# Three of every 24 high-part casts of a maxout MoE layer, cast by VectorE instead of ScalarE

## The chip, the cores and the metric

The kernel runs on one core of one Trainium2 chip. The metric is the device time of one execution in microseconds (us), the median of three runs. Five engines work side by side, each through its own queue in order: TensorE (PE, with its weight loads as PEld), VectorE (DVE), ScalarE (ACT), GpSimd (POOL) and SyncE (SP, which issues DMAs here).

## The reference

Four batches of 12,544 tokens with 128 channels go through attention over 32 inducing points, and then through a maxout layer:

```python
h = mab(I, x)          # 32 inducing points attend to the tokens
attn_out = mab(x, h)   # the tokens attend to the 32 results
x = attn_out.reshape(B * S, D)
h = np.maximum(np.maximum(x @ w1, x @ w2), x @ w3)   # 768 wide
return h @ w_out
```

`mab(q, kv)` is softmax(q kvT / sqrt(128)) kv. All of it is fp32.

## The kernel before

**What is computed.** The maximum is taken as x w2 + max(0, x (w1 - w2), x (w3 - w2)), so that x w2 w_out is one product with a 128 x 128 matrix. Since x itself is (probabilities) times a 32 x 128 matrix per batch, that small matrix is multiplied with all weights first (`us`, one per batch), and the tokens enter only through their transposed softmax probabilities `pT`, split in a high and a low part to keep fp32 accuracy.

**Tiling.** A batch has seven groups of tokens: a short one and six full ones of 16 x 128 tokens (groups 1 to 6). A full group is four chunks of 512 tokens. For each chunk the 768 hidden channels are six blocks of 128. One block of one chunk is a *slot*; a full group is a window of 24 slots, numbered 0 to 23 here (slot = 6 x chunk + block), and the kernel has 600 slots, 24 full windows among them. "b2 group 3" is the window of group 3 of the third batch; batches count from 0.

**One slot** passes through five engines' queues:
- PE multiplies `pu` (L790) and `pv` (L800) into PSUM, each of two banks in turn.
- ScalarE writes `ru` = max(0, pu) into SBUF (L809), which frees the bank of `pu`.
- VectorE writes `h` = max(pv, ru) (L830, from five buffers in turn), which frees the bank of `pv`.
- The high part `hi` of `h`, rounded to the type fp32r that PE reads in one pass, is a cast: on ScalarE (L819), or on VectorE (L817) for the slots of the whole kernel listed in `HIVEC` (0, 2, 4 and 7).
- The low part `lows` = h - hi is a subtraction: on POOL (L827), or on VectorE (L833) for the slots of a window listed in `LOWVEC` (23, 0, 15, 18; in the last batch `LOWLAST`, with 9 too; b0 group 1 only 23).
- Six slots later PE adds hi wo_hi, hi wo_lo and lows wo_hi into the chunk's accumulator (L862 to L864; one more product, L861, opens a chunk). After its sixth block ScalarE copies the chunk out of PSUM (L875) and SP stores it.

**What sets the order.** The order of each queue is the order in which the program calls the engines. `main()` walks over the slots; step s calls `advance()`, then what `plan[s]` holds, then `stage2()` for slot s - 6. `advance()` at step s issues pu of slot s + 1, pv of slot s, ru of s + 1, the high cast of slot s - 1, its low part on POOL, h of slot s, and last a low part that VectorE takes over from the step before. So the high cast of a slot stands just ahead of the next slot's h where VectorE does it, and behind the ru two slots on where ScalarE does it. `plan[s]` holds the rest of the work: the softmax of the coming group's probabilities in ten steps on VectorE and ScalarE (`STEPS2`, among them the exp of step 8 at L716, the division of step 11, the transposition of step 13 at L739 and the copy `ph` of step 14 at L742), and the attention of the inducing points of the next batch (products L366 and L502 in bursts on PE, exp L449, maxima L404 and L434, transposition L478). Batch 3 has no next batch, so there this attention is missing.

Of the kernel before, what the change touches and what calls it, by code (L numbers as in the profile page):

```python
# [25 lines left out]
def kernel(ctx, tc, x, xt, ind_t, w1, w2, w3, w_out, out):  # L26
# [6 lines left out]
    NJ = DF // P  # L33
# [85 lines left out]
    )  # L119
    LOWVEC = (23, 0, 15, 18)  # L120
    LOWLAST = (23, 0, 9, 15, 18)
    UW = 2 * DF + C
    UQ = UW // NQ

# [100 lines left out]
    wf = xtp.tile([P, 2, DF], F32, name="wf", tag="xT")  # L225
    wcat = const.tile([P, UW], F32, name="wcat")
    wo_hi = const.tile([P, NJ, C], F32R, name="wo_hi")
# [7 lines left out]
    def convert(k, step):  # L235

        v = raws[k].rearrange("p (k two) -> p two k", two=2)
        low, high = v[:, 0, :], v[:, 1, :]
        c = parts[k]
        if step == "t":  # L240
# [12 lines left out]
        elif step == "r":  # L253

            c["rest"] = temp(F32, "rest")
            nc.vector.scalar_tensor_tensor(
                out=c["rest"], in0=low, scalar=2.0**-52, in1=c["pw"].bitcast(F32), op0=ALU.mult, op1=ALU.mult
            )
        elif step == "z":

            c["size"] = temp(F32, "size")
            nc.scalar.activation(out=c["size"], in_=high.bitcast(F32), func=AF.Square)
        elif step in "Aa":
            (nc.gpsimd if step == "A" else nc.vector).tensor_add(out=c["rest"], in0=c["rest"], in1=c["t"].bitcast(F32))
        elif step == "d":

            c["dst"] = wf[:, k, :] if k < 2 else temp(F32, "dst")
            size, rest, dst = c["size"], c["rest"], c["dst"]
            if k != 1:

                size, rest = (v.rearrange("p (n two) -> p two n", two=2) for v in (size, rest))
                dst = dst.rearrange("p (two n) -> p two n", two=2)
            nc.vector.scalar_tensor_tensor(
                out=dst, in0=size, scalar=LEAST * LEAST, in1=rest, op0=ALU.is_ge, op1=ALU.mult
            )
        elif step == "S":
            nc.gpsimd.tensor_sub(
                out=wcat[:, : 2 * DF].rearrange("p (j s c) -> p s j c", s=2, c=P)[:, k - 2],
                in0=c["dst"].rearrange("p (j c) -> p j c", c=P),
                in1=wf[:, 0, :].rearrange("p (j c) -> p j c", c=P),  # L280
            )
# [333 lines left out]
    def first_products(st, which, bank):  # L615
        if which == 0:
            st["us"] = bp.tile([P, UW], F32R, name="us", tag="us")
            st["up"] = {}
        cs = slice(512 * which, min(UW, 512 * which + 512))
        up = bank[:, : cs.stop - cs.start]  # L620
# [25 lines left out]
    def combine_products(st, bank):  # L646
        st["us"] = bp.tile([P, UW], F32R, name="us", tag="us")
        st["up"] = bank
        for k in range(NQ):
            nc.tensor.matmul(  # L650
                out=bank[k * M : (k + 1) * M, :],
                lhsT=st["hT"][:, :M],
                rhs=wcat[:, k * UQ : (k + 1) * UQ],
                start=True,
                stop=True,
            )
# [20 lines left out]
    def turned(ap):  # L677

        return ap.rearrange("p (a b) -> p b a", a=2)

    def sorted_(ap):

        return ap.rearrange("p (b a) -> p a b", a=2)

    def halves(ap):

        return ap.rearrange("p (a b) -> p a b", a=2)
# [93 lines left out]
    HIVEC = (0, 2, 4, 7)  # L781

    def advance():

        s = pipe["next"]
        pipe["next"] += 1
        if s + 1 < len(slots):
            c, j = slots[s + 1]
            pu, w = bank_u[(s + 1) % 2], c.w
            nc.tensor.matmul(  # L790
                out=pu[:, :w],
                lhsT=state[c.b]["us"][:, 2 * j * P : (2 * j + 1) * P],
                rhs=turned(c.pT[:, :w]),
                start=True,
                stop=True,
            )
        if 0 <= s < len(slots):
            d, j = slots[s]
            pv = bank_v[s % 2]
            nc.tensor.matmul(  # L800
                out=pv[:, : d.w],
                lhsT=state[d.b]["us"][:, (2 * j + 1) * P : (2 * j + 2) * P],
                rhs=turned(d.pT[:, : d.w]),
                start=True,
                stop=True,
            )
        if s + 1 < len(slots):
            ru = hp.tile([P, 512], F32, name="ru", tag="ru", bufs=3)
            nc.scalar.activation(out=halves(ru[:, :w]), in_=sorted_(pu[:, :w]), func=AF.Relu)  # L809
            relus[s + 1] = ru  # L810
        low = pipe.pop("low", None)
        if 0 <= s - 1 < len(slots):
            c, j = slots[s - 1]
            h = sums.pop(s - 1)
            hi = hp.tile([P, 512], F32R, name="hi", tag="hi", bufs=10)
            if s - 1 in HIVEC:
                nc.vector.tensor_copy(out=hi[:, : c.w], in_=h[:, : c.w])  # L817
            else:
                nc.scalar.copy(out=hi[:, : c.w], in_=h[:, : c.w])  # L819
            lo = lows[:, (s - 1) % NL, :]  # L820
            c.hh.append(hi)
            c.hl.append(lo)
            args = dict(out=lo[:, : c.w], in0=h[:, : c.w], in1=hi.bitcast(F32)[:, : c.w])
            if c.low(j):
                pipe["low"] = args
            else:
                nc.gpsimd.tensor_sub(**args)  # L827
        if 0 <= s < len(slots):
            h = hp.tile([P, 512], F32, name="h", tag="h", bufs=5)
            nc.vector.tensor_max(out=halves(h[:, : d.w]), in0=sorted_(pv[:, : d.w]), in1=halves(relus.pop(s)[:, : d.w]))  # L830
            sums[s] = h
        if low:
            nc.vector.tensor_sub(**low)  # L833

    class Chunk:
# [7 lines left out]
        def low(self, k):  # L843

            if self.q is None or (self.gi == 1 and self.q == k == 0):
                return False
            if self.b == 0 and self.gi == 1:
                return NJ * self.q + k in LOWVEC[:1]
            return NJ * self.q + k in (LOWVEC if self.b + 1 < B else LOWLAST)

    def stage2(c, j):
        us = state[c.b]["us"]
        w = c.w
        if j == 0:
            c.acc = [(bank_o[c.n % 2], slice(0, w))]
            if c.n == len(chunks) - 1:
                c.acc = [(bank_a[k], slice(k * w // 2, (k + 1) * w // 2)) for k in range(2)]
        for acc, cs in c.acc:
            to = acc[:, : cs.stop - cs.start]
            if j == 0:  # L860
                nc.tensor.matmul(out=to, lhsT=us[:, 2 * DF :], rhs=turned(c.pT[:, cs]), start=True, stop=False)  # L861
            nc.tensor.matmul(out=to, lhsT=wo_hi[:, row_of(j), :], rhs=turned(c.hh[j][:, cs]), start=False, stop=False)  # L862
            nc.tensor.matmul(out=to, lhsT=wo_lo[:, row_of(j), :], rhs=turned(c.hh[j][:, cs]), start=False, stop=False)  # L863
            nc.tensor.matmul(out=to, lhsT=wo_hi[:, row_of(j), :], rhs=turned(c.hl[j][:, cs]), start=False, stop=(j == NJ - 1))  # L864
# [65 lines left out]
    def begins(win):  # L930
        b, g = divmod(win - 1, NG - 1)
        return b * per_batch + short + g * WIN

    for win, slot, kind, n, gi in MOVES:
        s = begins(win) + slot
# [39 lines left out]
    for n, turns in enumerate(TURNS, start=1):  # L975
        for gi, win, slot, wait, past in turns:
            s = begins(win) + slot
# [9 lines left out]
        s = begins(win) + (8 if slot < 8 else 20)  # L987
# [9 lines left out]
    def main():  # L997
        over = None
        for s in range(len(slots) + LAG + 1):

            if s >= LAG:
                spare[0] = bank_o[((s - LAG) // NJ + 1) % 2]
            if pipe["next"] <= s:
                advance()
            k = s // NJ + AHEAD
            if s % NJ == 4 and k < len(chunks):
                chunks[k].pT = probs(chunks[k])
            if over:
                finish(over)
                over = None  # L1010
            if s == len(slots) + LAG:
                break
            for f, args in plan[s]:
                f(*[state[a[1]] if isinstance(a, tuple) and a[0] == "state" else a for a in args])
            if s >= LAG:
                c, j = slots[s - LAG]
                stage2(c, j)
                if j == NJ - 1:
                    over = c

    def first(step, st):
# [18 lines left out]
            "eg": lambda: attend_products(1, 2, bank_a[1]),  # L1040
            "ek": lambda: keep_scores(1),
            "s": advance,
            "a": lambda: next(steps["a"]),
            "b": lambda: next(steps["b"]),
# [107 lines left out]
```

## Time and profile before

| what | value |
|---|---|
| median of three runs | 789.8 us (789.71 to 789.95) |
| the profiled execution's own time | 790.35 us |
| its span, first to last instruction | 788.5 us, granted TensorE clock 0.999 |
| busy share of the span | PE 98%, ACT 92%, DVE 81%, POOL 81%, PEld 79% |
| high casts on ScalarE, L819 | 596, of 128 x 512 elements 575 |
| high casts on VectorE, L817 | 4 |
| low parts on POOL, L827, and on VectorE, L833 | 504 and 96 |

A busy share counts overlapping instructions once; matmuls are pipelined, so that a PE which is always busy may still lose time between the starts of its matmuls. The rows below give an instruction's start in us from the span's start, its duration, engine, line, operation and operands. An engine's next instruction may start a little before the one ahead is over.

### The profile page before, as it was taken

To read this page: it belongs to the slowest core of one execution; us is meant where nothing else is said; L and a number is where in the kernel's file an instruction comes from. 1 tells how busy PE (TensorE), PEld (TensorE's weight loads), DVE (VectorE), ACT (ScalarE), POOL (GpSimd) and SP (SyncE) were. 2 spreads that over 40 slices of the span, in tenths; PEclk is the share of its full clock that TensorE was granted. 3 is DMA by queue.
4 is the path that set the end of the run, shared out by engine and by line. 5 is a ranking of instruction groups with operands and counts; after the bars stand their busy time and mean duration, and the time that the engine had idled before them with its cause. 6 is when DMAs were issued, how large, how long until landed. Compare 5 with 4: busy or idle time off the path is not lost.

```text
span 788.5 us, 14348 instructions
## 1 busy us (share of the span) xinstructions
PE 774.7 (98%) x4567; PEld 626.4 (79%) x4567; DVE 639.4 (81%) x1071; ACT 727.1 (92%) x1529; POOL 639.6 (81%) x523
## 2 busy tenths in 40 slices
PE   8999999999999999999999999999999999999998
PEld 6768878878787787787878877878888788787887
DVE  5898978878877787887887878878888788888876
ACT  5789899999998999998998999999999999999996
POOL 1379879878788897887987978879879989888887
PEclk9999999999999999999999999999999999999999
DMA  9744325274542643543644336334223222222221
GB/s 355 293 148 126 100 91 178 62 249 161 189 139 65 200 131 101 188 123 108 217 137 132 114 103 195 120 114 134 71 79 96 74 81 81 68 87 73 69 81 53
DMA packets 52266, 102.24 MB, mean 130 GB/s; under 512 B 18144, under 2 KB 21344, under 8 KB 46944
## 3 DMA queue, kind: packets, MB, share of 16 engines
q1 hardware_dynamic: 52048, 101.21, 40.5%
q8 instruction: 36, 0.59, 0.3%
q14 instruction: 38, 0.31, 0.1%
q10 hardware_dynamic: 144, 0.13, 0.0%
HBM read 48.12 MB, written 25.69 MB: 94 GB/s over the span
## 4 chain that ended last, share of the span: by engine, by line
PE 56%; ACT 33%; POOL 3%; DMA 3%; DVE 2%; issue 1%; SPq 0%; POOLq 0%; ACTq 0%; DVEq 0%
ACT ru L809 14%; ACT hi L819 13%; PE pu L790 10%; PE acc L862 9%; PE pv L800 9%; PE acc L863 9%; PE acc L864 9%; PE aux L696 3%; POOL lows L827 3%; ACT o L875 2%; PE acc L502 2%; DMA raw<-in_w_dram 2%; PE aux L366 2%; PE acc L861 2%; ACT aux L449 1%
## 5 line engine op out<-in xcount | busy, mean ns | idle before, releaser
L827 POOL TENSOR_TENSOR lows<-h,hi 128x512 fp32r<-128x512 f32 (+1 forms) x504 | 624.4, 1275 | 112.4 <-ACT hi L819 109.3
L830 DVE TENSOR_TENSOR h<-pv,ru 128x512 f32<-128x512 f32 (+1 forms) x600 | 400.9, 673 | 123.8 <-PE pv L800 63.0
L809 ACT ACTIVATE ru<-pu 128x512 f32<-128x512 f32 (+1 forms) x600 | 407.0, 679 | 37.8 <-PE pu L790 37.5
L819 ACT CAST hi<-h 128x512 fp32r<-128x512 f32 (+1 forms) x596 | 416.3, 699 | 0.3 <-DVE h L830 0.2
L790 PE MATMUL pu<-pT,us 128*128 128x512 f32 (+1 forms) x600 | 229.2, 382 | 4.5 <-ACT ru L809 3.7
L800 PE MATMUL pv<-pT,us 128*128 128x512 f32 (+1 forms) x600 | 226.6, 378 | 1.6 <-DVE h L830 1.5
L862 PE MATMUL acc<-hi,wo_hi 128*128 128x512 f32 (+1 forms) x594 | 225.5, 380 | 0.0
L863 PE MATMUL acc<-hi,wo_lo 128*128 128x512 f32 (+1 forms) x594 | 222.6, 375 | 0.0
L864 PE MATMUL acc<-lows,wo_hi 128*128 128x512 f32 (+1 forms) x594 | 222.6, 375 | 0.0
L790 PEld LDWEIGHTS pu<-pT,us 128*128 128x128 f32 x600 | 113.2, 189 | 37.8 <-ACT ru L809 18.8
L862 PEld LDWEIGHTS acc<-hi,wo_hi 128*128 128x128 f32 x594 | 112.2, 189 | 21.9 <-issue 7.5
L800 PEld LDWEIGHTS pv<-pT,us 128*128 128x128 f32 x600 | 113.4, 189 | 19.6 <-DVE h L830 6.6
L864 PEld LDWEIGHTS acc<-lows,wo_hi 128*128 128x128 f32 x594 | 112.3, 189 | 15.3
L863 PEld LDWEIGHTS acc<-hi,wo_lo 128*128 128x128 f32 x594 | 112.3, 189 | 14.7
L833 DVE TENSOR_TENSOR lows<-h,hi 128x512 fp32r<-128x512 f32 x96 | 87.7, 913 | 0.8 <-ACT hi L819 0.8
L875 ACT COPY o<-acc 128x512 f32<-128x512 f32 (+1 forms) x96 | 65.3, 680 | 0.0
L861 PE MATMUL acc<-pT,us 128*128 128x512 f32 (+1 forms) x99 | 37.3, 376 | 0.0
L502 PEld LDWEIGHTS acc<-xg,aT 128*32 128x32 f32 x640 | 18.0, 110 | 9.6 <-issue 5.4
L696 PE MATMUL aux<-xT,hT 128*32 128x512 f32 x192 | 25.1, 603 | 0.0
L366 PE MATMUL aux<-xT,iT 128*32 128x512 f32 x184 | 24.1, 596 | 0.2 <-ACT pT L768 0.2
L502 PE MATMUL acc<-xg,aT 128*32 128x128 f32 x640 | 21.4, 273 | 0.1
L861 PEld LDWEIGHTS acc<-pT,us 128*128 128x128 f32 x99 | 18.7, 189 | 2.6 <-DVE hs L540 0.2
(163 smaller groups left out, 445.6 us busy)
## 6 DMA issues: line engine op xcount, KB each, us to landing
out_dram<-o SPq DMA_DIRECT2D x95, 256.0 KB, 2.2
xg<-in_x_dram SPq DMA_DIRECT2D x23, 1024.0 KB, 6.1
xT<-in_xt_dram SPq DMA_DIRECT2D x18, 1024.0 KB, 5.5
pT<-ph SPq DMA_DIRECT2D x190, 64.0 KB, 2.0
pT<-pl SPq DMA_DIRECT2D x190, 64.0 KB, 2.0
raw<-in_w_dram SPq DMA_DIRECT2D x3, 768.0 KB, 8.7
us<-uh SPq DMA_DIRECT2D x24, 52.0 KB, 1.9
us<-ul SPq DMA_DIRECT2D x24, 52.0 KB, 2.5
```

What stands on the lines that cost most here:

```text
L790: nc.tensor.matmul(out=pu[:, :w], lhsT=state[c.b]["us"][:, 2 * j * P : (2 * j + 1) * P], rhs=turned(c.pT[:, :w]), start=True, stop=True,)
L800: nc.tensor.matmul(out=pv[:, : d.w], lhsT=state[d.b]["us"][:, (2 * j + 1) * P : (2 * j + 2) * P], rhs=turned(d.pT[:, : d.w]), start=True, ...
L809: nc.scalar.activation(out=halves(ru[:, :w]), in_=sorted_(pu[:, :w]), func=AF.Relu)
L819: nc.scalar.copy(out=hi[:, : c.w], in_=h[:, : c.w])
L827: nc.gpsimd.tensor_sub(**args)
L830: nc.vector.tensor_max(out=halves(h[:, : d.w]), in0=sorted_(pv[:, : d.w]), in1=halves(relus.pop(s)[:, : d.w]))
L833: nc.vector.tensor_sub(**low)
L861: nc.tensor.matmul(out=to, lhsT=us[:, 2 * DF :], rhs=turned(c.pT[:, cs]), start=True, stop=False)
L862: nc.tensor.matmul(out=to, lhsT=wo_hi[:, row_of(j), :], rhs=turned(c.hh[j][:, cs]), start=False, stop=False)
L863: nc.tensor.matmul(out=to, lhsT=wo_lo[:, row_of(j), :], rhs=turned(c.hh[j][:, cs]), start=False, stop=False)
L864: nc.tensor.matmul(out=to, lhsT=wo_hi[:, row_of(j), :], rhs=turned(c.hl[j][:, cs]), start=False, stop=(j == NJ - 1))
L875: copy(out=halves(o[:, :w]), in_=sorted_(acc[:, :w]))
```

## The change

In every full group, VectorE instead of ScalarE casts the high part of slots 7, 13 and 18. The method `high` of a chunk says so; the cast itself and its operands are the same. The low parts stay where they were.

```diff
     LOWLAST = (23, 0, 9, 15, 18)
+    HIGHVEC = (7, 13, 18)
...
-            if s - 1 in HIVEC:
+            if s - 1 in HIVEC or c.high(j):
                 nc.vector.tensor_copy(out=hi[:, : c.w], in_=h[:, : c.w])
             else:
                 nc.scalar.copy(out=hi[:, : c.w], in_=h[:, : c.w])
...
+        def high(self, k):
+
+            return self.q is not None and NJ * self.q + k in HIGHVEC
```

## Rows read from the trace of the kernel before

**Rows 1.** Busy time of b1 group 2; columns PE, PEld, DVE, ACT, POOL, clock, DMA, GB/s.
```profile
267.98:298.41 30.43, 30.12 (x173) 24.37 (x173) 24.86 (x41) 28.50 (x61) 25.15 (x21) 1.00 0.47 148
```
**Rows 2.** Waits of PEld in b1 group 2, from 50.66 to 612, and from 612.81: total, times, longest.
```profile
PEld pu L790 <- ACT ru L809: 1.1, 3, 0.7
...
PEld pu L790 <- ACT ru L809: 18.3, 47, 0.7
...
PEld pv L800 <- DVE h L830: 3.3, 5, 1.1
```
**Rows 3.** Timeline of PE in b1 group 2: start, us, engine, line, operation, tiles.
```profile
283.46 0.38 PE L800 MATMUL pv<-pT,us 128*128 128x512 f32 x1
...
290.15 0.38 PE L800 MATMUL pv<-pT,us 128*128 128x512 f32 x1
...
291.04 0.48 PE L790 MATMUL pu<-pT,us 128*128 128x512 f32 x1
...
295.89 0.38 PE L800 MATMUL pv<-pT,us 128*128 128x512 f32 x1
...
296.54 0.38 PE L864 MATMUL acc<-lows,wo_hi 128*128 128x512 f32 x1
297.23 0.48 PE L790 MATMUL pu<-pT,us 128*128 128x512 f32 x1 [0.31 <-ACT ru L809]
```
**Rows 4.** Timeline of ScalarE in b1 group 2.
```profile
282.13 0.66 ACT L819 CAST hi<-h 128x512 fp32r<-128x512 f32 x1
282.63 0.64 ACT L716 ACTIVATE aux<-aux 128x512 f32<-128x512 f32 x1
...
296.42 0.76 ACT L809 ACTIVATE ru<-pu 128x512 f32<-128x512 f32 x1
```
**Rows 5.** Timeline of VectorE in b1 group 2.
```profile
281.94 0.68 DVE L830 TENSOR_TENSOR h<-pv,ru 128x512 f32<-128x512 f32 x1
...
288.04 0.72 DVE L739 STREAM_TRANSPOSE aux<-aux 128x512 f32<-128x512 f32 x1
288.67 0.67 DVE L830 TENSOR_TENSOR h<-pv,ru 128x512 f32<-128x512 f32 x1
...
294.42 0.67 DVE L830 TENSOR_TENSOR h<-pv,ru 128x512 f32<-128x512 f32 x1
```
**Rows 6.** POOL in b1 group 2, merged, and all of L827: shortest, median, longest ns.
```profile
277.07 16.22 POOL L827 TENSOR_TENSOR lows<-h,hi 128x512 fp32r<-128x512 f32 x13 [1.77 <-ACT hi L819]
...
L827 POOL TENSOR_TENSOR lows<-h,hi x504: 729/1287/1765, 48.6 to 782.2; 128x512 fp32r<-128x512 f32 x160, 128x256 fp32r<-128x256 f32 x8
```
**Rows 7.** VectorE's casts and POOL early on, and all low parts on VectorE (L833).
```profile
49.69 0.73 POOL L827 TENSOR_TENSOR lows<-h,hi 128x256 fp32r<-128x256 f32 x1 [0.36 <-ACT hi L819]
49.71 0.86 DVE L817 CAST hi<-h 128x256 fp32r<-128x256 f32 x1
...
53.58 0.43 DVE L817 CAST hi<-h 128x512 fp32r<-128x512 f32 x1
53.70 2.68 POOL L827 TENSOR_TENSOR lows<-h,hi 128x512 fp32r<-128x512 f32 x2 [0.16 <-ACT hi L819]
...
L833 DVE TENSOR_TENSOR lows<-h,hi x96: 671/684/3627, 80.6 to 781.4; 128x512 fp32r<-128x512 f32 x96
```
**Rows 8.** Timelines of b0 group 1, by engine: VectorE, PE, POOL.
```profile
60.31 1.27 DVE L830 TENSOR_TENSOR h<-pv,ru 128x512 f32<-128x512 f32 x2
...
61.17 0.38 PE L800 MATMUL pv<-pT,us 128*128 128x512 f32 x1
...
53.70 22.56 POOL L827 TENSOR_TENSOR lows<-h,hi 128x512 fp32r<-128x512 f32 x18 [0.16 <-ACT hi L819]
```
**Rows 9.** Timelines of b3 group 2, by engine: VectorE, PE, POOL.
```profile
659.18 1.30 DVE L830 TENSOR_TENSOR h<-pv,ru 128x512 f32<-128x512 f32 x2
...
660.35 0.38 PE L800 MATMUL pv<-pT,us 128*128 128x512 f32 x1
...
645.90 16.76 POOL L827 TENSOR_TENSOR lows<-h,hi 128x512 fp32r<-128x512 f32 x13 [1.50 <-ACT hi L819]
```

## The prediction, made before the changed kernel was run

> **What bounds the kernel now.** I read the page's engine line first. With four engines nearly full the shares decide nothing, so I went to windows of 24 slots. Eight of the 24 last the same 30.43 us (b0 groups 3, 4; b1 and b2 groups 2 to 4); one of them stands for all [rows 1]. Then I asked who makes PE wait there: its weight loads wait 1.1 us, in three places, for ScalarE's `ru`, which must free a bank of `pu` [rows 2]. I read what this costs off PE's starts [rows 3], which step by 0.22 us: the pu that starts at 297.23 was due at 296.54 + 0.22 = 296.76, so 0.47 us is lost, and 0.10 more because a restarted matmul lasts 0.48 instead of 0.38 and the next starts that much later. The pu at 291.04 loses 0.02 and the same 0.10. In all **0.70 us a window**; the rest of PE's time is work that the change leaves alone.
>
> ScalarE's timeline says why [rows 4]. The high cast of slot 7 starts at 282.13 and the softmax exp right behind it, at 282.63: one cast takes 0.50 us of the queue (0.66 is its latency). Another exp, right behind slot 18's cast, pushes the next `ru` to 296.42, and the pu at 297.23 waits for that one. In batch 3 (from 612.81) the picture turns: PE's weight loads wait longest for VectorE's `h`, 3.3 us [rows 2].
>
> **The change, part by part.** 72 casts leave ScalarE, three a window: 3 x 0.50 = 1.50 us of its queue, two of them (1.0) ahead of the late `ru` at 291.04 and all three ahead of that at 296.42. This is more than the 0.47 and 0.02 lost there, so the ScalarE stalls go: 8 x 0.70 = 5.6 us. Elsewhere the weight loads wait 18.3 - 8 x 1.1 = 9.5 us for `ru` [rows 2]; at the same ratio (0.70 / 1.1) that is 6.0 us, nearly all in eight more windows (b0 groups 2, 5, 6; b1 groups 1, 5, 6; b2 groups 1, 6). **Given back: 11.6 us.**
>
> What VectorE takes on: the same cast took it 0.43 us at the start of the kernel [rows 7], some 0.34 of its queue, since its instructions start about 0.09 before the one ahead ends [rows 5]. No DMA and no semaphore partner beyond the changed engine is added; PE reads `hi` over 3 us later. But a cast stands in VectorE's order **ahead of the next slot's h**, and h frees the bank that pv two slots on needs. The cast's real price is a wait that the trace shows twice. The 256-wide cast at 49.71 took 0.86 us, twice what the 512-wide one took: POOL's subtraction had begun at 49.69 and ended at 50.42, and the cast ended 0.15 after that [rows 7]. The other way round, two subtractions that began at 53.70, under a cast that ended at 54.01, took 2.68 us [rows 7] where a pitch of 1.24 (16.22 less one, over 12) and a duration of 1.29 make 2.53 [rows 6]: 0.15 lost. So the two exclude each other, for their data phases: a cast caught by a POOL operation ends some 0.28 us after it, and costs POOL about 0.2. POOL runs 13 subtractions back to back from 277.07 [rows 6], over slots 7 and 13.
>
> [...]
>
> Now a steady window, cast by cast [rows 5, 6].
> - Slot 7: the cast can issue at 281.94, where `h` of slot 8 starts now. POOL's fourth of the 13 ends at 277.07 + 3 x 1.24 + 1.29 = 282.08 (about 282.1): no wait, `h` 0.38 late. Cover: that `h` ends at 282.62, and the pv that needs it starts at 283.46 [rows 3]. Cost nothing, but POOL is now 0.2 late.
> - Slot 13: the cast issues at 288.67, after the transposition at 288.04 (which hangs on PE, not on ScalarE). POOL's tenth starts at 277.07 + 9 x 1.244 + 0.20 = 288.47, 0.2 ahead of the cast, and ends at 289.76. The cast ends at 290.05, `h` of slot 14 starts at 289.97 instead of 288.67: **1.30 late**. It then ends at 290.64, and the pv that started at 290.15 [rows 3] starts at 290.69. With the restart: 0.64 lost.
> - Slot 18: the cast stands at 294.42, and by the same walk `h` there is up to 1.2 late; PE, already 0.64 later, needs that `h` for the pv that starts at 295.89 [rows 3], 0.8 after its present end at 295.09. Cover 1.4: nothing lost. Without the stall before it, up to 0.4 would show.
> Net in a steady window: -0.70 + 0.64 = -0.06; eight make **-0.5**.
>
> The eight others give back 6.0. I charge slot 14's 0.64 to four (b0 group 2, b1 group 5, b2 group 6, and one of the two group 1), and 0.27 for slot 8 to both group 1, whose cover there is short: 3.1. In b0 groups 5, 6 and b1 group 6 PE runs a burst of attention products over slot 14, which hides it. Net **-2.9**.
>
> b0 group 1 [rows 8]: VectorE bounds it. The cast issues at 60.31; POOL's subtraction there starts at 53.70 + 0.15 + 5 x 1.244 = 60.07, so the cast ends near 61.64, `h` 1.25 late, and pv at 61.17 moves by 1.1. The next two casts find no idle time on VectorE: 0.34 each and a wait between 0 and 1.2. Between 1.1 + 0.7 = 1.8 and 1.1 + 0.7 + 2.4 = 4.2 I take **+2.7**, as the waits are on average half of a POOL operation.
>
> Batch 3 [rows 9]: nothing to give back. In groups 1, 2 and 4 slot 13's cast issues at the 659.18 of `h`, some 0.4 behind POOL's eleventh start (13 in 16.76 us make a pitch of 1.29: 645.90 + 10 x 1.29 = 658.8): `h` 1.2 to 1.4 late, ending at 661.05 to 661.25, against a pv at 660.35: 0.7 to 0.9 lost, 0.1 restart and 0.1 from slot 7, about 1.0. Three make +3.0; group 6 I put at +0.4; in groups 3 and 5 POOL is idle there. **+3.4.**
>
> **Sum:** -0.5 - 2.9 + 2.7 + 3.4 = +2.7 us. The profiled execution took 790.35 (span 788.5 and 1.85 around it), so it would take 793.05; it stands 0.55 above the median of 789.8, so I predict 789.8 + 2.7 = **792.5 us**. Bounds: if no cast ever meets POOL, only b0 group 1 pays (3 x 0.34 = 1.0): 789.8 - 11.6 + 1.0 = 779.2. If each of the 15 costly casts (8 + 4 + 3) waits a whole POOL operation more (1.24): 792.5 + 18.6 = 811.1. What speaks for that end is one row: of 96 two-input subtractions of VectorE, which the same exclusion holds up, one took 3.63 us against a median of 0.68 [rows 7].
>
> **The rivals.** A change of under 0.2% (1.6 us) can't be told from none.
> - *Forecast, slower*: ScalarE's stalls are replaced by VectorE's waits on POOL. Chance 0.40.
> - *Faster*: at slot 14 the cast gets in before POOL's tenth subtraction. It decides at 288.67: POOL need only be 0.4 late instead of 0.2 by then (a longer hold by slot 7's cast), or VectorE 0.2 us earlier. Then the 0.64 goes in eight windows (5.1) and in three of the four others (1.9): 792.5 - 7.0 = 785.5. For it: the margin is 0.2 us, less than one cast. Against: POOL's order is regular and both starts hang on PE. Chance 0.28.
> - *No difference*: batch 3 and b0 group 1 pay half of my 6.1, as later idle time catches up: 792.5 - 3.0 = 789.5. For it: VectorE still has 30.43 - 24.86 = 5.6 us idle in a steady window [rows 1]. Chance 0.25.
> - [...] Chance 0.07, as most caught subtractions were served at once (the median is 0.68).
> The change can't fail to take effect: every full group has slots 7, 13 and 18.
>
> **How the numbers follow.** Range 784 to 797: the low end takes in the faster case with a margin of 1.5, the high end adds to 792.5 0.3 us in each of the 15 costly places; it leaves out the rest of the faster case (about 0.1) and the passed-over one. Forecast and passed-over are slower, 0.47; no difference 0.25; faster 0.28. The forecast's own range is 790.5 to 796.
>
> **What would show it.** VectorE's casts: shortest 0.43, mean near 0.9 us, the long ones at slot 13. The weight loads' waits of pu for `ru` fall from 18.3 us to under 4; those of pv for `h` in batch 3 rise from 3.3 [rows 2] to over 6. Steady windows stay near 30.4, b0 group 1 grows by about 2.7, batch 3 by 3.4 us. POOL's subtractions grow by 0.2 us some 50 times. Steady windows of 29.8 would show the forecast wrong, and the faster rival right.

## The result, and the profile after

The changed kernel takes **797.2 us** (median of four runs, 797.15 to 797.53) beside 789.9 us of the kernel before on the same chip: a ratio of 1.0094, with an interval of 1.0077 to 1.0111. It is slower, as forecast, but by 7.3 us where 2.7 were forecast, and the time lies 0.2 us beyond the upper end of the range of 784 to 797. The spans differ by 795.5 - 788.5 = 7.0 us; the granted clock stays at 0.999.

First the page: the engine line, then three groups of instructions (line, operands, count | busy us, mean ns | idle before them, and who ended it). All lines of the kernel moved by one: `pv` is L801, `h` L831, ScalarE's cast L820, POOL's low part L828, VectorE's L834; VectorE's cast is L818 (in the experiments' kernels they move by a few lines more).

```profile
PE 774.6 (97%) x4567; PEld 627.9 (79%) x4567; DVE 682.4 (86%) x1143; ACT 699.3 (88%) x1457; POOL 667.1 (84%) x523
...
L828 POOL TENSOR_TENSOR lows<-h,hi 128x512 fp32r<-128x512 f32 (+1 forms) x504 | 651.9, 1327 | 91.8 <-ACT hi L820 86.9
...
L820 ACT CAST hi<-h 128x512 fp32r<-128x512 f32 (+1 forms) x524 | 326.0, 622 | 20.5 <-DVE h L831 19.5
...
L818 DVE CAST hi<-h 128x512 fp32r<-128x512 f32 (+1 forms) x76 | 65.9, 868 | 2.0
```

72 casts have left ScalarE, which now stands idle 19.5 us until `h` comes. VectorE's casts last 868 ns on average, twice the 0.43 us of the free one in [rows 7].

Who makes PE wait? The weight loads' waits, from 51.0 to 614.94 (to the end of batch 2), and then in batch 3:

```profile
PEld pv L801 <- DVE h L831: 20.2, 35, 1.4
...
PEld pv L801 <- DVE h L831: 9.8, 16, 1.0
```

`pu` for `ru`, 18.3 us in 47 waits in [rows 2], is gone from the list. `pv` for `h` has its place, and in batch 3 that wait has grown from 3.3 to 9.8 us. So one wait took the place of another; the question is the size.

A steady window, b1 group 3, and b3 group 3, with the columns of [rows 1]:

```profile
300.35:330.71 30.36, 29.95 (x173) 24.55 (x172) 26.43 (x44) 27.04 (x57) 26.48 (x21) 1.00 0.42 125
672.04:701.90 29.86, 29.27 (x142) 23.61 (x141) 25.20 (x41) 26.80 (x53) 25.22 (x20) 1.00 0.24 71
```

The first took 30.44 before, the second 28.89. Inside the first, VectorE, POOL and PE around slot 13:

```profile
320.37 0.72 DVE L740 STREAM_TRANSPOSE aux<-aux 128x512 f32<-128x512 f32 x1
321.00 1.40 DVE L818 CAST hi<-h 128x512 fp32r<-128x512 f32 x1
322.32 1.27 DVE L831 TENSOR_TENSOR h<-pv,ru 128x512 f32<-128x512 f32 x2
...
320.81 2.72 POOL L828 TENSOR_TENSOR lows<-h,hi 128x512 fp32r<-128x512 f32 x2
...
322.27 0.38 PE L791 MATMUL pu<-pT,us 128*128 128x512 f32 x1
323.05 0.48 PE L801 MATMUL pv<-pT,us 128*128 128x512 f32 x1 [0.41 <-DVE h L831]
```

POOL's subtraction began at 320.81, 0.19 ahead of the cast; the cast took 1.40 us, and `h` of slot 14 started 1.32 late. The pv that needs the bank (of slot 16, two slots on) was due at 322.27 + 0.22 = 322.49 and started at 323.05: 0.56 lost, and 0.10 with the restart. The two subtractions took 2.72 us, where 2.53 was their time undisturbed [rows 6].

Window by window, after less before, and by the prediction's groups (each window from its first pu to the next window's first):

| group of windows | forecast, us | measured, us | the rows behind it |
|---|---|---|---|
| eight steady | -0.5 | +0.7 | five at -0.07 to -0.11; b1, b2 group 2 +0.48 and +0.49; b1 group 4 +0.19 |
| eight others | -2.9 | -1.5 | b1, b2 group 1 -0.83 and -0.85; b0 group 6 +0.58; b1, b2 group 6 +0.28 and +0.24 |
| b0 group 1 | +2.7 | +2.6 | |
| batch 3 | +3.4 | +4.8 | groups 1 to 5: +1.02, +0.98, +0.96, +0.62, +1.00; group 6 +0.25 |
| the rest | 0 | +0.3 | b2 group 5 and the short groups |
| sum | +2.7 | +6.9 | |

### The profile page after: what moved, and what is told of

The parts are those of the page before. It is cut to its first block, busy times and chain, and to the rows that moved or that the text cites. A ratio compares the mean times of both kernels' runs of the same rounds, so it can differ in the third digit from the quotient of the medians.

```text
span 795.5 us, 14417 instructions
## 1 busy us (share of the span) xinstructions
PE 774.6 (97%) x4567; PEld 627.9 (79%) x4567; DVE 682.4 (86%) x1143; ACT 699.3 (88%) x1457; POOL 667.1 (84%) x523
## 4 chain that ended last, share of the span: by engine, by line
PE 72%; ACT 15%; DVE 7%; DMA 3%; issue 2%; POOL 1%; SPq 0%; POOLq 0%; DVEq 0%; ACTq 0%
PE pv L801 13%; PE acc L867 12%; PE acc L868 12%; PE acc L869 12%; PE pu L791 12%; ACT ru L810 6%; ACT hi L820 6%; DVE h L831 4%; PE aux L697 3%; PE acc L503 2%; PE acc L866 2%; DMA raw<-in_w_dram 2%; PE aux L367 2%; ACT o L880 1%; ACT ph L743 1%
## 5 line engine op out<-in xcount | busy, mean ns | idle before, releaser
L828 POOL TENSOR_TENSOR lows<-h,hi 128x512 fp32r<-128x512 f32 (+1 forms) x504 | 651.9, 1327 | 91.8 <-ACT hi L820 86.9
L831 DVE TENSOR_TENSOR h<-pv,ru 128x512 f32<-128x512 f32 (+1 forms) x600 | 393.8, 670 | 90.3 <-PE pv L801 64.7
L810 ACT ACTIVATE ru<-pu 128x512 f32<-128x512 f32 (+1 forms) x600 | 364.0, 608 | 49.9 <-PE pu L791 49.6
L820 ACT CAST hi<-h 128x512 fp32r<-128x512 f32 (+1 forms) x524 | 326.0, 622 | 20.5 <-DVE h L831 19.5
L801 PE MATMUL pv<-pT,us 128*128 128x512 f32 (+1 forms) x600 | 230.1, 384 | 11.8 <-DVE h L831 11.6
L791 PE MATMUL pu<-pT,us 128*128 128x512 f32 (+1 forms) x600 | 225.2, 376 | 0.1
L801 PEld LDWEIGHTS pv<-pT,us 128*128 128x128 f32 x600 | 113.3, 189 | 45.3 <-DVE h L831 30.0
L834 DVE TENSOR_TENSOR lows<-h,hi 128x512 fp32r<-128x512 f32 x96 | 83.0, 864 | 0.8 <-ACT hi L820 0.8
L818 DVE CAST hi<-h 128x512 fp32r<-128x512 f32 (+1 forms) x76 | 65.9, 868 | 2.0
L880 ACT COPY o<-acc 128x512 f32<-128x512 f32 (+1 forms) x96 | 58.0, 604 | 0.0
```

Source lines behind the costliest of these rows:

```text
L791: nc.tensor.matmul(out=pu[:, :w], lhsT=state[c.b]["us"][:, 2 * j * P : (2 * j + 1) * P], rhs=turned(c.pT[:, :w]), start=True, stop=True,)
L801: nc.tensor.matmul(out=pv[:, : d.w], lhsT=state[d.b]["us"][:, (2 * j + 1) * P : (2 * j + 2) * P], rhs=turned(d.pT[:, : d.w]), start=True, ...
L880: copy(out=halves(o[:, :w]), in_=sorted_(acc[:, :w]))
```

## The experiments

Two theories stood against each other. **W**: the price is the wait of VectorE's cast for a running POOL subtraction, ahead of the next slot's `h`. **L**: the price is VectorE's longer queue alone, wherever POOL stands. Diffs are against the changed kernel; window differences are against the kernel before, ratios with their 95% intervals likewise. The experiments ran on several chips, so a time is compared with that of the kernel before on its own chip (789.9 to 790.5 us).

**One slot at a time.** Three kernels, `HIGHVEC` with one entry each:

```diff
-    HIGHVEC = (7, 13, 18)
+    HIGHVEC = (7,)
...
+    HIGHVEC = (13,)
...
+    HIGHVEC = (18,)
```

> Only slot 7 is cast by VectorE. Theory W (a cast waits for POOL's running subtraction, and the next slot's h stands behind it): in the steady windows this cast issues as a subtraction ends, so h is 0.4 us late under a cover of 0.8 and PE loses nothing, while ScalarE's queue is 0.5 us shorter before both late ru: 0.6 us less per steady window. b0 group 1 pays 1.2, batch 3 some 0.5. About 782.5 us, VectorE's casts 0.43 to 0.5 us in the steady windows. Rival L (what costs is the 0.34 us of VectorE's queue, wherever it stands and whatever POOL does): a third of the change's +7.3, so about 792.3 us.

784.3 us, 0.9924 (0.9905 to 0.9944): faster than both kernels, 1.8 above W's number and 8.0 below L's. The steady windows gain 0.50 each. One row of VectorE in b1 group 3 shows the cast that meets no POOL operation:

```profile
309.61 0.47 DVE L818 CAST hi<-h 128x512 fp32r<-128x512 f32 x1
```

> Only slot 13 is cast by VectorE. Theory W: the cast is caught by a subtraction that began 0.4 us before it (POOL is not yet late), takes about 1.15 us, h of slot 14 is 1.1 late against a cover of 0.8: 0.43 lost per steady window against 0.70 of ScalarE stalls given back; five windows of batch 3 lose 0.8 each, b0 group 1 loses 1.0. About 791 us, the dearest of the three. Rival L: 792.3 us, the same as for the other two.

789.7 us, 0.9998 (0.9982 to 1.0015): no change, 1.3 below W's number and 2.6 below L's. In the steady windows ScalarE's stall of 0.70 is replaced by a wait of `pv` for the `h` of slot 14, 0.34 + 0.10; seven of the eight gain 0.26 to 0.30. In the eighth, b2 group 3, the cast waited for two POOL subtractions, and the window loses 0.96:

```profile
504.79 2.42 DVE L818 CAST hi<-h 128x512 fp32r<-128x512 f32 x1
```

Groups 1, 2 and 4 of batch 3 lose 0.83, 0.77 and 0.42; groups 3 and 5 lose nothing (-0.08 both).

> Only slot 18 is cast by VectorE. Theory W: h of slot 19 is 0.75 us late under a cover of 0.75 to 0.8, so next to nothing is lost, and the late ru behind the exp comes 0.5 us earlier: some 0.5 less per steady window, the 0.12 at slot 18 stays. About 784 us. Rival L: 792.3 us.

792.2 us, 1.0028 (1.0017 to 1.0038). W missed by 8 us and L's number is met, but not for L's reason: L would lengthen all windows, and the steady ones gain 0.40 to 0.48. Group 6 of b0 and b1 pays 0.96 and 0.80, and b0 group 1 alone 3.53. There, VectorE's, POOL's and PE's timelines:

```profile
72.40 3.94 DVE L818 CAST hi<-h 128x512 fp32r<-128x512 f32 x1
76.26 2.04 DVE L831 TENSOR_TENSOR h<-pv,ru 128x512 f32<-128x512 f32 x3
...
53.53 22.53 POOL L828 TENSOR_TENSOR lows<-h,hi 128x512 fp32r<-128x512 f32 x18 [0.16 <-ACT hi L820]
76.42 3.77 POOL L828 TENSOR_TENSOR lows<-h,hi 128x512 fp32r<-128x512 f32 x3 [0.36 <-DVE hi L818]
...
77.00 0.48 PE L801 MATMUL pv<-pT,us 128*128 128x512 f32 x1 [3.23 <-DVE h L831]
```

This cast didn't wait for one subtraction but for all that POOL had: POOL's run ends at 53.53 + 22.53 = 76.06, the cast at 76.34. It was passed over, as the 3.63 us low part in [rows 7] was. Such a wait is worth three of the usual ones.

The traced run is one of two that took 790.5 us, at a granted clock of 1.000; the six others took 792.0 to 793.6 at 0.995 to 0.998. One stretch of 3.4 us at half the clock, as the relief run below shows it, would cost some 1.7 us and bring the mean to 0.998: an estimate, as those six left no trace. Medians against the kernel before, slot by slot: -6.1, -0.6 and +1.9 us, together -4.8 (the traced spans: -6.6, -1.1 and -0.1, together -7.8); the three casts together make +7.3. **The parts don't add.**

**Is it the delay of `h`?** VectorE casts behind the next slot's `h`, not ahead of it:

```diff
-            if s - 1 in HIVEC or c.high(j):
+            behind = c.high(j)
+            if behind:
+                cast = dict(out=hi[:, : c.w], in_=h[:, : c.w])
+            elif s - 1 in HIVEC:
...
+        if behind:
+            nc.vector.tensor_copy(**cast)
+            if "low" not in pipe:
+                nc.gpsimd.tensor_sub(**args)
```

> The same 72 casts on VectorE, but each behind the next slot's h in VectorE's order instead of ahead of it (POOL's subtraction of that slot is called behind the cast as well). Theory W: the casts still wait for POOL (mean 0.8 us and more), but what they now delay is the h one slot on, by 0.4 to 0.9 us under covers of 0.9 to 1.3, so the pv waits at slots 8 and 14 go: steady windows fall to 29.75 us, the total to about 783 us, b0 group 1 still pays about 2. Rival L: VectorE's queue holds as much as before, so 797 us within 1.

798.8 us, 1.0109 (1.0092 to 1.0126): W missed by 16 us, and L's number is near, but not for L's reason. The wait for the `h` of slot 14 is gone, and slot 18's cast is now the one caught (VectorE, then the weight loads' waits, b1 group 3):

```profile
326.31 1.28 DVE L838 CAST hi<-h 128x512 fp32r<-128x512 f32 x1
...
PEld pv L801 <- DVE h L835: 0.9, 2, 0.7
```

The stall moved to the first slots of the next window; the steady windows stand at -0.10, as with the change. Moving the casts by one place didn't help here; another one was caught.

**The two halves.** One kernel leaves the three casts out altogether (relief):

```diff
...
+            if c.high(j):
+                hi = last_hi[0]
...
```

The other makes VectorE cast into a tile that nobody reads, while ScalarE goes on casting (load):

```diff
...
+            if c.high(j):
+                nc.vector.tensor_copy(out=unread[:, : c.w], in_=h[:, : c.w])
+            if s - 1 in HIVEC:
...
```

> ScalarE's 72 casts are gone and nobody does them: for slots 7, 13 and 18 the high part of the slot before stands in for the slot's own, so 72 casts are left out; all else is as in the changed kernel. This is the gain alone. Theory W with the prediction's count: ScalarE's stalls go, 11.6 us, so about 778 us, steady windows 29.7 us. Rival R (ScalarE's stalls only hide other waits, so that its relief is worth little): over 786 us.

> ScalarE casts all slots as in the kernel before, and VectorE casts slots 7, 13 and 18 once more, at the changed kernel's place, into a tile that nobody reads. This is the cost alone. Theory W: the stalls of pv for h are those of the changed kernel (0.65 per steady window at slot 14, 1.0 in batch 3, 2.6 in b0 group 1, some 15 us in all), and ScalarE's stalls at slot 23 partly stay: 800 to 808 us. Theory L gives about the same here; the run sizes the cost.

Load: 799.2 us, 1.0113 (1.0093 to 1.0133), 0.8 below what was expected. Its steady windows stand at -0.02 although ScalarE's queue is as full as before. The weight loads' waits of b1 group 3 say why:

```profile
PEld pv L802 <- DVE h L834: 0.8, 1, 0.8
...
PEld pu L792 <- ACT ru L811: 0.3, 2, 0.2
```

While PE waits for the `h` of slot 14, ScalarE catches up: the 1.1 us that PE waited for it in [rows 2] are down to 0.3. **The two stalls of one window don't add.** With the casts' waits in place, relieving ScalarE is worth 799.2 - 797.2 = 2.0 us, or 1.5 if each is taken against the kernel before on its own chip, and the two intervals overlap; in any case far from the 11.6 that the stalls summed to.

Relief alone: 801.8 us, 1.0145 (1.0120 to 1.0171), where 778 was expected. Rival R's "over 786" is met, but its reason is not what the windows show. Some do as W expected: b0 group 4 and b1 group 3 gain 0.74 and 0.75, and in the latter neither pu nor pv waits at all. But five windows lose 3.3 us, and two more 1.6 and 1.8. In the first of the five, b0 group 3, VectorE, POOL, PE and four stretches by engine (columns as in [rows 1]):

```profile
131.04 3.96 DVE L841 TENSOR_TENSOR lows<-h,hi 128x512 fp32r<-128x512 f32 x1
...
119.53 14.92 POOL L835 TENSOR_TENSOR lows<-h,hi 128x512 fp32r<-128x512 f32 x12
...
135.66 0.63 PE L802 MATMUL pv<-pT,us 128*128 128x512 f32 x1 [2.12 <-DVE mx L435]
136.09 0.63 PE L874 MATMUL acc<-hi,wo_hi 128*128 128x512 f32 x1
...
133.30:135.60 2.30, 0.23 (x2) 0.00 (x0) 2.30 (x4) 0.00 (x0) 1.16 (x1) 1.00 0.96 378
135.90:139.20 3.30, 3.30 (x9) 2.55 (x9) 2.30 (x5) 2.74 (x7) 1.29 (x1) 0.50 0.23 76
139.40:142.00 2.60, 2.60 (x14) 2.28 (x13) 1.86 (x3) 2.19 (x5) 2.11 (x2) 1.00 0.00 0
```

Here it is VectorE's own low part of slot 15 that is passed over until POOL's run ends, at 119.53 + 14.92 = 134.45. PE stands still from 133.4 to 135.66, and then its granted clock is 0.50: from 136.09 its matmuls step by 0.43 instead of 0.22 us, until 139.2. Two prices in one event: the stall of 2.3 us, and behind it eight steps that take 0.21 longer, 1.7 us. In the two windows that lose 1.6 and 1.8 (b2 groups 4 and 6) the low part of slot 15 is passed over just so, but the clock stays at 1.00 and the second price is not paid.

**Without the cast.** The high part made by a second maximum of `pv` in PSUM and `ru` in SBUF:

```diff
...
+            if d.high(j2):
+                highs[s] = hi2 = hp.tile([P, 512], F32R, name="hi", tag="hi", bufs=10)
+                nc.vector.tensor_max(out=halves(hi2[:, : d.w]), in0=sorted_(pv[:, : d.w]), in1=halves(r[:, : d.w]))
...
```

> Slots 7, 13 and 18: VectorE makes the high part not by a cast from SBUF but by a second maximum of pv (PSUM) and ru, written as fp32r right behind h. [...] Theory W: no wait for POOL (each 0.68 us, none over 0.8), h of the next slot 0.6 late under covers of 0.8, no pv stall in steady windows (29.75 us); batch 3 loses some 0.25 in five windows, b0 group 1 about 1.8: about 782 us. POOL's subtractions no longer grow from 1.29 to 1.47. Rival L: VectorE's queue carries 72 x 0.6 = 43 us instead of 25, so slower than the changed kernel, over 800 us.

Three runs took 817.3, 817.4 and 822.8 us, 1.0366 (1.0329 to 1.0402). It was to be the fastest and is the slowest. (The traced execution took 830.6, so only the mechanism is read from it.) All second maxima took 0.67 to 0.68 us (first line: shortest, median, longest in ns): as W said, none of them waited for POOL. What W left out is another operation. VectorE, POOL and PE in b1 group 2:

```profile
L841 DVE TENSOR_TENSOR hi<-pv,ru x72: 672/680/682, 59.6 to 815.8; 128x512 fp32r<-128x512 f32 x72
...
303.60 3.95 DVE L843 TENSOR_TENSOR lows<-h,hi 128x512 fp32r<-128x512 f32 x1
...
299.55 7.46 POOL L833 TENSOR_TENSOR lows<-h,hi 128x512 fp32r<-128x512 f32 x6
...
308.81 0.48 PE L803 MATMUL pv<-pT,us 128*128 128x512 f32 x1 [2.71 <-DVE hi L841]
...
309.71 0.64 PE L878 MATMUL acc<-lows,wo_hi 128*128 128x512 f32 x1
```

The same event as with relief: the low part of slot 15 waits until POOL's run is over (307.01), PE stands idle for 2.7 us, and from 309.7 its matmuls take 0.64 instead of 0.38. It comes in ten windows, eight of which lose 3.9 us; so L's "over 800" is met by these windows, not by a longer queue in all.

**Is POOL the cause?** POOL leaves out the low parts of slots 11 and 12 of each full group, so that it stands idle when slot 13 is cast. Its control is the same omission in the kernel before.

```diff
-            else:
+            elif c.q is None or NJ * c.q + j not in (11, 12):
                 nc.gpsimd.tensor_sub(**args)
```

> The changed kernel, but POOL leaves out the low parts of slots 11 and 12 of every full group (the products that read them find what the buffers held), so that POOL stands idle when VectorE casts slot 13. By the theory that the casts' waits for POOL cost the time: slot 13's cast takes 0.43 to 0.6 us instead of 1.27 to 1.40, the pv stall at slot 14 goes, a steady window takes 29.7 to 29.8 us instead of 30.3, groups 1 to 5 of batch 3 grow by 0.2 to 0.3 instead of 1.0, total 785 to 789 us. By the theory that VectorE's longer queue alone costs it: 797 us as with the change, since VectorE has the same work.

> The control for the run without POOL's low parts of slots 11 and 12: the same omission in the kernel before. If POOL's operations matter to the changed kernel only through VectorE's casts, the kernel before does not gain by the omission: 789.0 to 790.5 us, steady windows 30.4 us with ScalarE's stalls of 0.70 in them. If POOL's load alone costs both kernels: 784 to 787 us. VectorE's low part of slot 15 could meet POOL at another phase, which would move single windows by up to 1 us.

784.5 us, 0.9927 (0.9913 to 0.9942): 12.7 us less than the changed kernel, 0.5 below W's numbers and 12.5 from L's. The control: 789.4 us, 0.9985 (0.9975 to 0.9994), and its steady windows are those of the kernel before to 0.01 us. So POOL's load alone costs the kernel some 1 us; the rest of the 12.7 it costs through what VectorE does beside it, the casts first and its low parts of slot 15, which run free here too. VectorE, POOL and the windows of b1 group 3 and b3 group 3:

```profile
317.02 0.72 DVE L740 STREAM_TRANSPOSE aux<-aux 128x512 f32<-128x512 f32 x1
317.64 0.41 DVE L818 CAST hi<-h 128x512 fp32r<-128x512 f32 x1
317.98 1.27 DVE L831 TENSOR_TENSOR h<-pv,ru 128x512 f32<-128x512 f32 x2
...
306.05 11.44 POOL L828 TENSOR_TENSOR lows<-h,hi 128x512 fp32r<-128x512 f32 x9 [2.33 <-ACT hi L820]
318.13 2.67 POOL L828 TENSOR_TENSOR lows<-h,hi 128x512 fp32r<-128x512 f32 x2 [0.64 <-DVE hi L818]
...
297.00:326.69 29.69, 29.69 (x174) 24.69 (x173) 25.01 (x44) 27.07 (x57) 23.39 (x19) 1.00 0.44 139
662.29:691.30 29.01, 29.01 (x141) 23.62 (x140) 24.33 (x41) 26.69 (x53) 22.77 (x18) 1.00 0.25 73
```

POOL's run ends at 317.49, the cast comes at 317.64 and takes 0.41, `h` of slot 14 isn't held up, and the window is 0.75 shorter than before: the whole of ScalarE's stall (0.70) is back. Seven of the eight steady windows do so; in b1 group 4 slot 7's cast is caught (1.35 us) and it loses 0.21. b3 group 3 is 0.12 longer than before instead of 0.96. VectorE did the same work as with the change. L falls, and W stands as to the cause; what W did not foretell in four of the runs above is which operation POOL catches next.

**A version that beats both?** Casts from b0 group 2 to the end of batch 2 only: of slot 7; of 7 and 18; of 7 and 13 behind the next `h` (as above).

```diff
-    HIGHVEC = (7, 13, 18)
+    HIGHVEC = (7,)
...
         def high(self, k):
+            if not (0 < self.b < 3 or self.b == 0 and self.gi > 1):
+                return False
```

> VectorE casts slot 7 alone, and only from b0 group 2 to the end of batch 2 (there is a ScalarE stall to take away there). Slot 7 alone gave 784.3 us, with +0.93 in b0 group 1 and +0.2 to +0.3 in batch 3. Both theories: these go, 783.0 to 783.8 us, the windows in between as with slot 7 alone (steady ones 29.9).

> VectorE casts slots 7 and 18, from b0 group 2 to the end of batch 2. If casts cost only where they hold up the next h: steady windows -0.50 to -0.70, group 6 of batches 0 and 1 +0.6 (slot 18's cast caught at a POOL operation's start), total 782 to 785 us. If an earlier ScalarE lets POOL run without a gap and so pass over VectorE's operations: one or more windows longer by over 3 us, total above 786.

> VectorE casts slots 7 and 13, each behind the next slot's h instead of ahead of it, from b0 group 2 to the end of batch 2. If only the delay of h costs: no pv stall at slot 14, steady windows 29.7 to 29.9 us, total 780 to 783. If a ScalarE that is no longer late lets POOL run without a gap until it passes over a VectorE operation for several of its own: windows longer by over 3 us with a granted clock below 1 behind the stall, total 795 to 805.

784.1 us, 0.9923 (0.9906 to 0.9939); 788.4 us, 0.9984 (0.9972 to 0.9995); 787.3 us, 0.9966 (0.9954 to 0.9978). The first is slot 7 alone again (784.3): b0 group 1 is free of its 0.93, but group 2 behind it takes 1.1 more (a low part of VectorE takes 3.63 us there, passed over, instead of 2.39). The other two fit neither expectation: 788.4 is above 786, but no window lost over 3 us, and most steady ones gained 0.26 to 0.30 where slot 7 alone gains 0.50. So an earlier ScalarE alone doesn't bring about that VectorE is passed over. In both one stall has moved: with 7 and 18, VectorE in b1 group 3 reads

```profile
321.98 1.67 DVE L834 TENSOR_TENSOR lows<-h,hi 128x512 fp32r<-128x512 f32 x1
...
324.35 0.73 DVE L818 CAST hi<-h 128x512 fp32r<-128x512 f32 x1
```

where the low part of slot 15 is caught (0.67 us when free) and the cast of slot 18 comes late after it; PE's weight loads then wait 0.7 us for `h`, in two places. So slot 7 alone, everywhere or in the middle, is the best that was run: 6 us under the kernel before and some 13 under the change.

## Where the prediction was wrong, and where it was right

The sign and the mechanism came true, the size did not: 7.3 us instead of 2.7. The step that failed is the walk to the costly places. The prediction counted 15. In batches 0 to 2, b0 group 1 aside, it priced only the waits for the `h` of slots 8 and 14, and it put slot 18's cast, the low parts on VectorE and two groups of batch 3 at nothing. Its range allowed 0.3 us more in each of the 15 and nothing for a place outside the list. The runs showed waits outside it, one by one below.

- **What bounded the kernel: right.** ScalarE's stalls are gone with its casts; without POOL in the way seven of the eight steady windows gave back 0.74 or 0.75, against 0.70 read off PE's starts.
- **The steady window, cast by cast: right.** Slot 7 waits for nobody (0.46 us); slot 13 is 0.19 behind POOL's start (0.2 forecast), `h` 1.32 late (1.30), 0.56 + 0.10 lost (0.54 + 0.10); slot 18's cast took 0.72 and cost nothing. Five windows came out at -0.09 (forecast -0.06). The faster rival, decided by that 0.2 us, fell with it.
- **"Eight make -0.5": wrong by 1.2 us.** I took each window as closed. b1 and b2 group 2 begin with a stall that group 1 hands on. VectorE, POOL before; VectorE, POOL and PE after, across that border:

```profile
265.76 0.77 DVE L833 TENSOR_TENSOR lows<-h,hi 128x512 fp32r<-128x512 f32 x1
...
267.32 5.01 POOL L827 TENSOR_TENSOR lows<-h,hi 128x512 fp32r<-128x512 f32 x4 [1.34 <-ACT hi L819]
```
```profile
267.53 1.81 DVE L834 TENSOR_TENSOR lows<-h,hi 128x512 fp32r<-128x512 f32 x1
...
261.91 11.05 POOL L828 TENSOR_TENSOR lows<-h,hi 128x512 fp32r<-128x512 f32 x8
...
270.00 0.48 PE L801 MATMUL pv<-pT,us 128*128 128x512 f32 x1 [0.19 <-DVE h L831]
```

  Before, ScalarE was late, so POOL stood idle for 1.34 us while VectorE took slot 18's low part in 0.77. After, ScalarE is early, POOL runs through, and the same low part takes 1.81. I had counted the casts' waits. That POOL holds up VectorE's low parts too stood in the prediction, but only as one row for the upper bound; in the sum it was put at nothing, without a look at what happens when ScalarE comes earlier: **its lateness had been keeping POOL out of the low parts' way.** Against the forecast of -0.06 each, the two group 2 windows make 1.1 of the 1.2; b1 group 4 (+0.19), where slot 7's cast was caught instead, makes 0.25, and the five others give 0.2 back.
- **"Net -2.9" for the eight others: -1.5.** The step that failed is the one that charged group 6 of b0 and b1 nothing because PE's burst covers slot 14. It does; but slot 18's cast, behind the burst, came just as a POOL subtraction started. VectorE and PE in b0 group 6:

```profile
231.17 1.52 DVE L818 CAST hi<-h 128x512 fp32r<-128x512 f32 x1
...
233.35 0.48 PE L801 MATMUL pv<-pT,us 128*128 128x512 f32 x1 [0.59 <-DVE h L831]
```

  The cast took 1.52 us and PE lost 0.75 + 0.10. With an equal share of the 6.0 given back to each window, group 6 of b0 and b1 came out 2.4 us dearer than forecast, and b0 group 5 and b2 group 6 0.8. Errors the other way hid 1.8 of this: b0 group 2 and group 1 of b1 and b2 came out cheaper. In neither group 1 was slot 13's cast caught (0.42 us), so the 0.64 charged to one of them was not paid. That the miss is only 1.4 is luck.
- **b0 group 1: right**, +2.63 against +2.7, by a middle value: the waits of its second and third cast were put anywhere from 0 to 1.2 each, 1.2 together, and came to 0.9 and 0.5 (casts of 1.34 and 0.94 us against 0.43 undisturbed).
- **Batch 3: 4.8, not 3.4.** Groups 1 and 2 cost 1.0 each, as worked out, and group 4 0.6. (By its own rows `h` there is 1.1 to 1.3 late, 0.1 less than the prediction wrote.) That "in groups 3 and 5 POOL is idle there" is the step that failed, for +0.96 and +1.00. VectorE and POOL of the kernel before in b3 group 3, then of the changed one:

```profile
687.99 1.30 DVE L830 TENSOR_TENSOR h<-pv,ru 128x512 f32<-128x512 f32 x2
...
686.78 2.55 POOL L827 TENSOR_TENSOR lows<-h,hi 128x512 fp32r<-128x512 f32 x2
```
```profile
692.31 1.27 DVE L818 CAST hi<-h 128x512 fp32r<-128x512 f32 x1
...
692.03 1.27 POOL L828 TENSOR_TENSOR lows<-h,hi 128x512 fp32r<-128x512 f32 x1
```

  POOL was not idle; the first of those two subtractions was 0.07 us from its end when VectorE came by at 687.99 (686.78 + half of 2.55 = 688.06). With slot 13 alone the cast there takes 0.41 us (at 686.86) and the group loses nothing:

```profile
686.86 0.41 DVE L818 CAST hi<-h 128x512 fp32r<-128x512 f32 x1
```

  With slot 7's cast as well, counted from the window's first pu, VectorE comes 0.18 later (at 20.27 us, against 20.09 with slot 13 alone) and POOL's next subtraction starts 0.14 earlier (19.99 against 20.13). So the cast comes 0.28 behind that start, and pays in full.
- **The sum.** 1.2 + 1.4 - 0.1 + 1.4 + 0.3 = 4.2 us more than forecast. The mechanism, the sign and the price per caught cast held; which operations are caught did not. The same mistake stands in the forecast for POOL: 50 times 0.2 = 10 us, against 651.9 - 624.4 = 27.5 us more busy time (the latter from the page's group before). By the trace some 12 of it stand at VectorE's casts, and some 16 at its low parts, which now meet POOL more often.
- **Passed over**, that is, an operation of VectorE waits for more than the one subtraction it meets (chance 0.07), didn't come in the changed kernel (its longest cast took 1.52 us, its longest low part 1.81), but it is the largest part of why the expectations for slot 18 alone, for relief and for the second maximum missed. "No difference" failed with batch 3.

## What to carry to other kernels

In these kernels a cast from SBUF to SBUF that VectorE took over lasted 0.41 to 0.47 us where no GpSimd subtraction was running as it arrived, and up to 1.52 in the changed kernel where one was; VectorE's subtractions of two SBUF tiles lasted 0.67 us free and up to 1.81 there, and its maxima of a PSUM and an SBUF tile never more than 0.70. So look where both engines stand at that moment, and if the margin is smaller than the time you are adding ahead of it, charge the full wait. Stalls on different engines need not add up, and neither need the gains from removing them: relieving ScalarE, with the casts' waits in place, was worth 1.5 to 2.0 us where its stalls were put at 11.6. An engine that comes earlier can close the gaps in which others were served: at the border to b1 group 2 POOL's idle 1.34 us went, and a low part of VectorE took 1.81 us instead of 0.77. So after each step walk all operations that were seen to wait for GpSimd, not only the new ones. Where a change has several parts, time them one at a time: here one of the three was worth 6 us, and all three cost 7.3.

## What the runs showed of the hardware

- **VectorE's casts and low parts and POOL's subtractions held each other up.** In the changed kernel the caught 512-wide casts ended 0.28 to 0.29 us after the POOL operation ahead of them (692.03 + 1.27 = 693.30, the cast at 693.58), and the caught two-input low parts some 0.55 after it, as in the relief run (134.45 and 135.00). The two subtractions around slot 13's cast took 2.72 us where 2.53 was their time undisturbed.
- **In a few cases VectorE was passed over.** Over the fourteen traces 496 of VectorE's casts and low parts began with more than 0.2 us left of a POOL subtraction and another behind it within 0.12 us. None of them ended before that subtraction; 469 waited for it alone, and 27 (11 in the psum run, 9 in the relief run, at most 1 in any other) for one or two more. The longest took 3.9 to 4.1 us; three of these, shown above, ended only when POOL had run dry: VectorE, held up, made no more `h`, and in the relief run POOL then stood idle for 3.10 us until the next `hi`. What decides it stays open: the start of the low part within POOL's operation doesn't, since in the relief run one at 0.340 us into it was passed over, and another at 0.346 us was not.
- **A maximum of a PSUM and an SBUF tile didn't wait.** VectorE's 72 second maxima of `pv` (PSUM) and `ru` (SBUF) in the psum run took 0.67 to 0.68 us, and none of the 600 `h` of the same form took over 0.70 us in any trace, POOL running or not.
- **Behind some stalls of PE the granted clock fell.** In the relief run seven stalls of PE lasted 2.2 to 2.3 us; behind five of them the granted clock was 0.50 for 3.4 us, and behind the two others, which end at 557.60 and 618.23, it stayed at 1.00. In the psum run it fell behind nine of ten stalls of 2.9 to 3.0 us (in b1 group 2 to a mean of 0.56 from 310.2 to 313.2). Behind the stall that ends at 77.00 in the traced run of slot 18 alone, the longest of all (3.4 us), it stayed at 1.00, as it did behind all stalls in the windows of the changed kernel (up to 1.1 us). So it didn't fall behind every long stall, and no run here shows what decides.
